# Attention with a window, then a gated feed-forward: earlier requests for V and q/k, weights between casts, inverse sums first

## The chip, the cores and the metric

The kernel runs on one core of a Trainium2 chip. The metric is the device time of one execution in microseconds, as the median of several runs. A core has four computing engines that run side by side and meet at semaphores: TensorE (PE, matrix products; its weight loads are listed apart as PEld), VectorE (DVE), ScalarE (ACT) and GpSimd (POOL). SyncE (SP) only asks for transfers. ScalarE and GpSimd can ask for transfers too. [...]

## The reference

There are 4 batches of 8 heads, 768 positions and 64 values per head. A query sees the 128 positions up to its own and the first 4 positions ("sinks"). The heads' outputs are put side by side as 512 columns and go through a gated feed-forward.

```python
scores = scale * np.matmul(q, k.transpose(0, 1, 3, 2))
keep = is_sink | in_window            # pos < 4, or 0 <= i - j < 128
a = np.exp(where(keep, scores, -1e9) - max)
a = a / (sum(a) + 1e-09)
x = matmul(a, v)                      # -> (3072, 512)
out = (maximum(x @ w_gate, 0) * (x @ w_val)) @ w_out   # 512 -> 1536 -> 512
```

All inputs and the output are float32. The kernel computes in bfloat16 with float32 sums.

## The kernel before

Two heads form a pair; a batch has 4 pairs, `U[0]` to `U[3]` for batch 0. For a pair the kernel does three things:

- **T**: transposes q and k on TensorE (for batch 0 in halves of 384 positions, `T_half(c)`: `c` 0 to 3 are the first halves of pairs 0 to 3, 4 to 7 the second halves) and copies them out of PSUM.
- **S**: scores, `Sg(u, s)`, for a group `s` of query blocks, exp on ScalarE and, where no bias was added, a mask product on VectorE. Groups 0 and 3 serve the first half of the positions, 4 and 2 the second half, in batch 0.
- **V**: `V(u, part)`, for a half of the positions: sums of the exps (weights `ones`), the weighted sums over V (weights `vn`), the inverse, and the product of both into `xT`.

V has 7 row blocks `j`; part 0 needs `j` 0 to 2 and 16 rows of 3, part 1 needs 2 to 6. The first part of the program is the *head*: everything up to the first half of the positions of batch 0, all 4 pairs.

```python
def load_half(c, queues=(nc.sync, nc.sync)):     # asks for half c of k and of q
def cast_half(c, copies=(gpsimd, gpsimd)):       # to bfloat16, k and q
def gate_half(c):
    nc.gpsimd.memset(half(kf, c)[0:1, 0:2], 0.0) # the load that follows waits for GpSimd to get here
def load_w(m0, m1):                              # one request each for w_gate and w_val, on GpSimd's queue
...
def T_half(c):
    t, x = c % NP, c // NP
    if c <= NP:
        both = pair()                            # one PSUM tile for k and q
        tk, tq = both[:, 0, :], both[:, 1, :]
    else:
        tk, tq = G[3][:, 0:256], G[3][:, 256:512]
    ... 6 transposes (line 260), key copies on ScalarE (line 266)
    (nc.scalar.copy if c in (2, 3, 4) else nc.vector.tensor_copy)(qT..., vq)     # line 267

def V(u, part, between=None):
    pv, pd = two()
    ...
    sums(pd, lambda j, h: ones[:])               # line 301
    if between:
        between()
    sums(pv, lambda j, h: vn[u.b % 2][:, j, 2 * u.p + h, :])   # line 301
    nc.vector.transpose(out=t1[:], in_=pd[:, 0:CUT])           # line 312
    nc.vector.reciprocal(r[:], ...)
    nc.vector.transpose(out=R..., in_=r...)
    nc.vector.tensor_tensor(xT..., pv[:, 0:CUT], R[:], op=Alu.mult)   # line 316
...
# the head, its second half
V(U[0], 0, lambda: T_half(2))
cast_half(3, (nc.gpsimd.tensor_copy, nc.scalar.copy))
Sg(U[2], 0)
load_w(0, 2)
V(U[1], 0)
Sg(U[2], 3)
T_half(3)
cast_half(4)
V(U[2], 0)
Sg(U[3], 0)
cast_half(5)
Sg(U[3], 3)
for c in (6, 7):
    gate_half(c)
    load_half(c)
load_w(2, 4)
T_half(4)
V(U[3], 0)
load_w(4, 6)
Sg(U[0], 4)
T_half(5)
Sg(U[0], 2)
spin(3, 2)                                       # idle matmuls that keep TensorE going
```

Behind the head come 96 *slots*, 24 for each batch: a slot is one chunk `(b, g, m)` of the feed-forward's first layer, that is 4 matmuls for the gate (line 328), relu on ScalarE, 4 matmuls for the value (line 333) and a product on VectorE into `hT` (line 335). Chunk `m` uses weights `m`. Behind each chunk stand the pieces of attention that the plan gives to its slot, and three matmuls of the second layer (line 348) where they are ready. Ahead of each chunk stands what `prep` gives to its slot: casts and requests.

```python
for s, w in {0: "S14 S12", 2: "H2", 3: "S24 S22 H3", 5: "S34 S32", 6: "V01", 7: "V11", 8: "V21", 9: "V31"}.items():
    ...                       # S14: Sg of pair 1, group 4; H2: second half of pair 2 transposed; V01: pair 0, part 1
for s, w in {11: "T0", 12: "T1", 13: "S00 S01", ..., 22: "V30 S02"}.items():   # batch 1
    ...
prep[0] += [("half", 6), ("lv0",), ("w", 6, 8), ("half", 7), ("w", 8, 10)]     # casts of halves 6, 7; weights
prep[2] += [("v", 0, j) for j in (3, 4, 5, 6)]                                 # casts of V 3 to 6
prep[3] += [("w", 10, 12)]
prep[7] += [("load", 4), ("load", 5), ("load", 6), ("lv", 1)]                  # loads of batch 1
```

Here `lv0` first writes two values of each of V's blocks 3 to 6 on GpSimd, so that the requests for them, on SyncE, wait for GpSimd to get to this place.

Of the kernel before, what the change touches and what calls it, by code (L numbers as in the profile page):

```python
# [19 lines left out]
def kernel(  # L20
# [12 lines left out]
    nc = tc.nc  # L33
    B, H, S, D = q.shape
    assert (B, H, S, D) == (4, 8, 768, 64)
    NP = H // 2
# [13 lines left out]
    NQ, NE, NT = 3, 4, 4  # L50
# [34 lines left out]

    V2 = [(4, 2, 0, 255, 112), (5, 2, 255, 399, 240), (6, 2, 399, 419, 364)]
    VSEG = [[(0, 0, 0, 247, 0), (1, 0, 247, 499, 120), (2, 1, 0, 140, 244), (3, 1, 255, 267, 372)],
            [(2, 1, 140, 255, 0), (3, 1, 267, 507, 0)] + V2]
    VSEG0 = [[(0, 0, 0, 247, 0), (1, 0, 247, 499, 120), (2, 1, 0, 140, 244), (3, 1, 140, 152, 372)],
             [(2, 1, 152, 267, 0), (3, 1, 267, 507, 0)] + V2]  # L90

    class Unit:
        def __init__(self, i):
# [2 lines left out]
    U = [Unit(i) for i in range(B * NP)]  # L96
# [15 lines left out]
    def cast_half(c, copies=(nc.gpsimd.tensor_copy, nc.gpsimd.tensor_copy)):  # L112
        for src, dst, copy in ((kf, kn, copies[0]), (qf, qn, copies[1])):
            copy(half(dst, c).rearrange("p (n h d) -> p h n d", n=3, h=2),
                                  half(src, c).rearrange("p (h n d) -> p h n d", n=3, h=2))

    def gate_half(c):
        nc.gpsimd.memset(half(kf, c)[0:1, 0:2], 0.0)


    VROW = [0, 116, 244, 368, 496, 620, 748]
# [52 lines left out]
    def setup():  # L174
        nc.vector.memset(warm[:], 0.0)
        nc.scalar.activation(warm[:], warm[:], Act.Exp, bias=0.0, scale=1.0)
        make_identity(nc, ident)

        nc.gpsimd.memset(band[:], 1.0)
        nc.gpsimd.affine_select(out=band[:], in_=band[:], compare_op=Alu.is_ge, fill=0.0, base=0,  # L180
                                pattern=[[1, 256]], channel_multiplier=-1)
        nc.gpsimd.affine_select(out=band[:], in_=band[:], compare_op=Alu.is_ge, fill=0.0, base=127,
                                pattern=[[-1, 256]], channel_multiplier=1)
        nc.gpsimd.affine_select(out=msk[:, 0, 0:247], in_=band[:, 0:247], compare_op=Alu.is_ge, fill=0.0,
                                base=119, pattern=[[0, 247]], channel_multiplier=-1)
        cp, ms = nc.vector.tensor_copy, nc.vector.memset
        for i in range(NT):
            ms(kE[i][:, 120:124], 0.0)
            ms(kE[i][:, 396:508], 0.0)
            ms(kE[i][:, 784:896], 0.0)  # L190
        ms(ones[:], 1.0)
        ms(vn[0][:, 3, :, :], 0.0)
        cp(msk[:, 0, 247:499], band[:, 4:256])
        ms(msk[0:4, 0, 247:499], 1.0)
        ms(msk[0:4, 0, 0:120], 1.0)
        ms(msk[0:4, 0, 120:247], 0.0)
        bias(mb[:, 0, 0:499], msk[:, 0, 0:499])
        bias(mb[:, 1, 0:140], band[:, 0:140])
        bias(mb[:, 1, 140:152], band[:, 4:16])
        ms(mb[0:4, 1, 140:152], 0.0)  # L200
        ms(vf[:, 6, :, :], 0.0)

    def bias(dst, src):
        nc.vector.tensor_scalar(dst, src, -1.0, BIG, op0=Alu.add, op1=Alu.mult)

    def setup2():
        cp, ms = nc.vector.tensor_copy, nc.vector.memset
        for g, w in ((1, 252), (2, 144)):
            cp(msk[:, g, 0:255], band[:, 0:255])
            cp(msk[:, g, 255:255 + w], band[:, 4:4 + w])  # L210
            ms(msk[0:4, g, 255:255 + w], 1.0)
        cp(msk[:, 2, 399:419], band[:, 0:20])

    rot, srot = [0], [0]
    head = [True]
# [34 lines left out]

    def T_half(c):
        t, x = c % NP, c // NP
        if c <= NP:
            both = pair()
            tk, tq = both[:, 0, :], both[:, 1, :]
        else:
            tk, tq = G[3][:, 0:256], G[3][:, 256:512]
        for src, ps in ((kn, tk), (qn, tq)):
            for n in range(3):
                nc.tensor.transpose(ps.bitcast(BF16)[:, 128 * n:128 * n + 128], half(src, c)[:, 128 * n:128 * n + 128],  # L260
                                    ident[:])
        vk, vq = (ps.bitcast(BF16)[:, 0:HALF].rearrange("d (n p) -> d p n", p=128) for ps in (tk, tq))
        e = kE[t]

        for r0, r1, c0 in ((0, 40, 0), (40, 124, 128), (124, 128, 384)) if x == 0 else ((0, 80, 396), (80, 128, 640)):
            nc.scalar.copy(e[:, c0:c0 + 3 * (r1 - r0)].rearrange("d (p n) -> d p n", n=3), vk[:, r0:r1])
        (nc.scalar.copy if c in (2, 3, 4) else nc.vector.tensor_copy)(
            qT[t][:, x * HALF:x * HALF + HALF].rearrange("d (p n) -> d p n", n=3), vq)
        if x == 0:
            sinks(U[t], nc.scalar.copy)  # L270
# [20 lines left out]

    ready = {}

    def V(u, part, between=None):
        pv, pd = two()
        segs = (VSEG if u.b else VSEG0)[part]

        def sums(out, w):
            for i, (j, g, c0, c1, o0) in enumerate(segs):
                for h in range(2):  # L300
                    nc.tensor.matmul(out=out[64 * h:64 * h + 64, o0:o0 + c1 - c0], lhsT=w(j, h),  # L301
                                     rhs=ee[u.i % NE][:, g, h, c0:c1], start=i == 0, stop=i == len(segs) - 1,
                                     skip_group_check=True)

        sums(pd, lambda j, h: ones[:])
        if between:
            between()
        sums(pv, lambda j, h: vn[u.b % 2][:, j, 2 * u.p + h, :])
        t1 = npool.tile([128, CUT], F32, name="t1")
        R = npool.tile([128, CUT], F32, name="R")  # L310
        r = npool.tile([128, CUT // 32], F32, name="r")
        nc.vector.transpose(out=t1[:], in_=pd[:, 0:CUT])  # L312
        nc.vector.reciprocal(r[:], t1[:].rearrange("p (c e) -> p c e", e=32)[:, :, 0])
        nc.vector.transpose(out=R[:].rearrange("p (c e) -> p c e", e=32),  # L314
                            in_=r[:].unsqueeze(2).to_broadcast([128, CUT // 32, 32]))
        nc.vector.tensor_tensor(xT[u.b % 2][:, u.p, CUT * part:CUT * part + CUT], pv[:, 0:CUT], R[:], op=Alu.mult)  # L316
        ready[u.b, u.p, part] = True

    gvn = [0]

# [34 lines left out]
    with tc.manual_schedule():  # L355
# [9 lines left out]
        for c in range(3, 6):  # L365
            load_half(c)
        setup()
        cast_half(0)
        T_half(0)
        spin(5)  # L370
        cast_half(1)
        T_half(1)
        setup2()
        Sg(U[0], 0)
        Sg(U[0], 3)
        cast_v(0, 0)
        spin(2)
        Sg(U[1], 0)
        cast_v(0, 3, 16, nc.vector.tensor_copy)
        cast_half(2)  # L380
        cast_v(0, 1)
        cast_v(0, 2)
        Sg(U[1], 3)
        V(U[0], 0, lambda: T_half(2))
        cast_half(3, (nc.gpsimd.tensor_copy, nc.scalar.copy))
        Sg(U[2], 0)
        load_w(0, 2)
        V(U[1], 0)
        Sg(U[2], 3)
        T_half(3)  # L390
        cast_half(4)
# [1 line left out]
        Sg(U[3], 0)  # L393
        cast_half(5)
        Sg(U[3], 3)
        for c in (6, 7):
            gate_half(c)
            load_half(c)
        load_w(2, 4)
        T_half(4)  # L400
        V(U[3], 0)
        load_w(4, 6)
        Sg(U[0], 4)
        T_half(5)
        Sg(U[0], 2)
        spin(3, 2)
        head[0] = False


# [8 lines left out]
            at[st] = s  # L418
            plan[s].append(st)

        for s, w in {0: "S14 S12", 2: "H2", 3: "S24 S22 H3", 5: "S34 S32", 6: "V01", 7: "V11", 8: "V21",
                     9: "V31"}.items():
            for y in w.split():
                put(s, y, 0)
        for s, w in {11: "T0", 12: "T1", 13: "S00 S01", 14: "S10 S11", 15: "T2", 16: "S20 S21", 17: "V00", 18: "V10",
                     19: "T3", 20: "V20", 21: "S30 S31", 22: "V30 S02"}.items():
            for y in w.split():
                put(s, y, 1)
        for b in range(2, B + 1):
# [5 lines left out]
            for x, y in enumerate(w.split()):  # L435
                put(24 * (b - 1) + x // 2 * 2, y[0] + y[2:], b - (y[1] == "p"))
        prep = [[] for _ in slots]
        prep[0] += [("half", 6), ("lv0",), ("w", 6, 8), ("half", 7), ("w", 8, 10)]
        prep[2] += [("v", 0, j) for j in (3, 4, 5, 6)]
        prep[3] += [("w", 10, 12)]  # L440
        prep[7] += [("load", 4), ("load", 5), ("load", 6), ("lv", 1)]
        prep[9] += [("kq", 4)]
        prep[10] += [("load", 7), ("kq", 5)]
        prep[13] += [("kq", 6)]
        prep[14] += [("v", 1, j) for j in range(7)]
        prep[16] += [("kq", 7), ("td", 8), ("wo",)]
        for i in range(ND, len(U)):
            t = at["S", i - NP, 2] + 1
# [12 lines left out]
        for s, (b, g, m) in enumerate(slots):  # L461
            for x in prep[s]:
# [12 lines left out]
                elif x[0] == "td":  # L475
                    to_dram(U[x[1]])
                elif x[0] == "turn":
                    turn(U[x[1]])
                elif x[0] == "sinks":
                    sinks(U[x[1]], nc.gpsimd.tensor_copy)  # L480
                elif x[0] == "lv0":
                    for j in (3, 4, 5, 6):
                        nc.gpsimd.memset(vf[32:33, j, 0, 0:2], 0.0)
                        load_v(0, j, 16 if j == 3 else 0)
                elif x[0] == "lv":
                    for j in range(7):
                        load_v(x[1], j)
                else:
                    cast_v(*x[1:])
# [55 lines left out]
```

The softmax here doesn't subtract the row's maximum and nothing guards it: scores larger than these inputs give would overflow.

## Time and profile before

| | |
|---|---|
| time, median of 3 | 265.59 us (265.55 to 266.02) |
| span of the profiled execution | 264.3 us |
| start of chunk 0 | 20.51 us |
| TensorE, busy | 249.9 us, 95% |
| VectorE, ScalarE, GpSimd, busy | 149.1, 117.4, 74.0 us |
| Sync queue (q1), moved | 21.83 MB |
| GpSimd queue (q0), moved | 7.87 MB |
| granted TensorE clock, mean | 0.986 |

In a line of a timeline the columns are: start, duration, engine, line of the program, instruction, what it writes and reads with shapes, and how many instructions are merged; in brackets the idle time ahead of it and what ended that. A wait for several things is put down to the one that came last by the profile, which is sometimes not the true one. "Busy" of PE and PEld overlap.

### The profile page before, as it was taken

What the parts mean: (1) busy time and instruction counts of PE and PEld (TensorE: products, weight loads), DVE (VectorE), ACT (ScalarE), POOL (GpSimd) and SP (SyncE); (2) the same over time, 40 slices, a digit from 0 to 9 for tenths busy, and PEclk for the clock granted to TensorE, in tenths of its full rate; (3) what the DMA queues carried; (4) which work ended last, traced back from release to release, by engine and by line L of the source; (5) the groups of instructions that cost most, each with busy time, mean ns of one, the idle gap of its engine ahead of it and who ended that gap; (6) DMA issues with size and microseconds to landing.
All of it is one profiled execution on the core that took longest, in us unless ns stands there. A gap on an engine that the chain in (4) does not pass through costs nothing.

```text
span 264.3 us, 5502 instructions
## 1 busy us (share of the span) xinstructions
PE 249.9 (95%) x2145; PEld 140.6 (53%) x2145; DVE 149.1 (56%) x314; ACT 117.4 (44%) x226; POOL 74.0 (28%) x106
## 2 busy tenths in 40 slices
PE   7889939998989999999999999999999999999994
PEld 3465515655646555555555555555555655555441
DVE  5577718777986774666537667657355642322000
ACT  3777802386353535553434355464344233332211
POOL 6687135299920014694000044000000000000000
PEclk9999968999999999999999999999999999999999
DMA  7999999939999259499412395310110111001232
GB/s 191 255 192 215 189 300 278 190 120 71 191 169 140 56 134 198 97 166 160 93 46 62 61 218 112 93 40 2 40 42 0 42 40 41 28 16 40 79 122 79
DMA packets 81266, 30.45 MB, mean 115 GB/s; under 512 B 65368, under 2 KB 77144, under 8 KB 81240
## 3 DMA queue, kind: packets, MB, share of 16 engines
q1 hardware_dynamic: 47944, 21.83, 33.3%
q0 software_dynamic: 32752, 7.87, 31.8%
q8 instruction: 17, 0.28, 0.5%
q10 hardware_dynamic: 544, 0.39, 0.5%
q14 instruction: 9, 0.07, 0.1%
HBM read 28.48 MB, written 9.44 MB: 143 GB/s over the span
## 4 chain that ended last, share of the span: by engine, by line
PE 77%; DMA 9%; DVE 4%; POOL 3%; issue 2%; SPq 2%; ACT 2%; ACTq 0%; POOLq 0%; DVEq 0%
PE g L348 21%; PE g L328 21%; PE g L333 20%; PE pp L301 7%; DMA vf<-in_v_dram 6%; PE pp L348 4%; PE pp L282 4%; DMA qf<-in_q_dram 4%; SPq L130 2%; DVE hT L335 1%; PE pp L240 1%; POOL vn L134 1%; DVE qT L248 1%; ACT ee L286 1%; DVE R L314 1%
## 5 line engine op out<-in xcount | busy, mean ns | idle before, releaser
L335 DVE TENSOR_TENSOR hT<-gs,g 128x384 bf16<-128x384 f32 x96 | 52.9, 551 | 64.9 <-PE g L333 63.1
L331 ACT ACTIVATE gs<-g 128x384 f32<-128x384 f32 x96 | 47.4, 494 | 76.9 <-PE g L328 75.7
L333 PE MATMUL g<-xT,wv 128*128 128x384 bf16 x384 | 78.8, 328 | 1.0 <-ACT ee L286 0.6
L328 PE MATMUL g<-xT,wg 128*128 128x384 bf16 x384 | 79.0, 328 | 0.0
L348 PE MATMUL g<-wo,hT 128*128 128x512 bf16 x240 | 64.1, 380 | 0.0
L286 ACT ACTIVATE ee<-pp 128x998 bf16<-128x998 f32 (+4 forms) x52 | 45.7, 903 | 31.3 <-PE pp L282 31.0
L328 PEld LDWEIGHTS <-wg 128*128 128x128 bf16 x384 | 36.1, 98 | 31.7 <-issue 1.2
L333 PEld LDWEIGHTS <-wv 128*128 128x128 bf16 x384 | 37.5, 98 | 27.1 <-DMA wv<-in_moe_w_val_dram 2.1
L348 PEld LDWEIGHTS <-hT 128*128 128x128 bf16 x288 | 26.2, 98 | 26.2 <-issue 2.1
L289 DVE TENSOR_TENSOR ee<-ee,msk 128x838 bf16<-128x838 bf16 (+4 forms) x48 | 29.3, 619 | 8.8 <-ACT ee L286 8.6
L134 POOL CAST vn<-vf 128x512 bf16<-128x512 f32 x28 | 17.8, 653 | 39.6 <-DMA vf<-in_v_dram 39.6
L151 POOL DMA_DIRECT2D qd<-in_q_dram x8 | 25.1, 4248 | 0.0
L151 POOL DMA_DIRECT2D kd<-in_k_dram x8 | 22.7, 3676 | 0.3 <-issue 0.3
L312 DVE STREAM_TRANSPOSE t<-pp 128x384 f32<-128x384 f32 x28 | 16.3, 581 | 8.9 <-PE pp L301 8.3
L352 ACT COPY ot<-g 128x512 f32<-128x512 f32 x20 | 11.7, 585 | 18.2 <-PE g L348 17.4
L282 PE MATMUL pp<-qT,kE 64*128 64x255 bf16 (+6 forms) x240 | 17.4, 246 | 2.0 <-DVE qT L248 1.0
L314 DVE STREAM_TRANSPOSE R<-r 128x384 f32<-128x384 f32 x32 | 18.5, 578 | 1.1
L301 PE MATMUL pp<-ee,vn 128*64 128x115 bf16 (+8 forms) x256 | 14.5, 236 | 4.2 <-POOL vn L134 4.2
L301 PEld LDWEIGHTS <-ones 128*64 128x64 bf16 x288 | 12.3, 110 | 9.7 <-issue 9.4
L316 DVE TENSOR_TENSOR xT<-pp,R 128x384 bf16<-128x384 f32 x28 | 15.6, 557 | 1.0
L301 PEld LDWEIGHTS <-vn 128*64 128x64 bf16 x288 | 12.5, 111 | 5.5 <-POOL vn L134 5.4
L301 PE MATMUL pp<-ee,ones 128*64 128x115 bf16 (+8 forms) x256 | 14.5, 239 | 0.1
(76 smaller groups left out, 126.7 us busy)
## 6 DMA issues: line engine op xcount, KB each, us to landing
out_dram<-ot SPq DMA_DIRECT2D x24, 256.0 KB
vf<-in_v_dram SPq DMA_DIRECT2D x12, 256.0 KB
vf<-in_v_dram SPq DMA_DIRECT2D x12, 224.0 KB
kf<-in_k_dram SPq DMA_DIRECT2D x8, 192.0 KB
wg<-in_moe_w_gate_dram POOLq DMA_DIRECT2D x6, 256.0 KB, 7.2
wv<-in_moe_w_val_dram POOLq DMA_DIRECT2D x6, 256.0 KB, 8.9
kf<-in_k_dram SPq DMA_DIRECT2D x4, 384.0 KB
qf<-in_q_dram SPq DMA_DIRECT2D x4, 384.0 KB
```

Of the source, the lines that this page charges most:

```text
L134: copy(flat(vn[b % 2][0:rows, j, :, :]), flat(vf[0:rows, j, :, :]))
L151: nc.gpsimd.dma_start(out=dst[u.i - ND].rearrange("s (h d) -> s h d", h=2), in_=x[u.b, 2 * u.p:2 * u.p + 2].rearrange("h s d -> s h d"))
L282: nc.tensor.matmul(out=ps[:, h, c0:c1], lhsT=kE[t][64 * h:64 * h + 64, x0:x0 + 128], rhs=qT[t][64 * h:64 * h + 64, q0:q0 + c1 - c0], start ...
L286: nc.scalar.activation(x, ps[:, :, b0:n], Act.Exp, bias=0.0, scale=scale)
L289: nc.vector.tensor_tensor(x, x, msk[:, g, m0:m0 + c1 - c0].unsqueeze(1).to_broadcast([128, 2, c1 - c0]), op=Alu.mult)
L301: nc.tensor.matmul(out=out[64 * h:64 * h + 64, o0:o0 + c1 - c0], lhsT=w(j, h), rhs=ee[u.i % NE][:, g, h, c0:c1], start=i == 0, stop=i == l ...
L314: nc.vector.transpose(out=R[:].rearrange("p (c e) -> p c e", e=32), in_=r[:].unsqueeze(2).to_broadcast([128, CUT // 32, 32]))
L328: nc.tensor.matmul(out=gp[:, 0:CUT], lhsT=wg[:, ko, m * 128:(m + 1) * 128], rhs=x[:, ko, c], start=ko == 0, stop=ko == KO - 1)
L331: nc.scalar.activation(gs[:], gp[:, 0:CUT], Act.Relu, bias=0.0, scale=1.0)
L333: nc.tensor.matmul(out=vp[:, 0:CUT], lhsT=wv[:, ko, m * 128:(m + 1) * 128], rhs=x[:, ko, c], start=ko == 0, stop=ko == KO - 1)
L335: nc.vector.tensor_tensor(h[:, m, c], gs[:], vp[:, 0:CUT], op=Alu.mult)
L348: nc.tensor.matmul(out=op, lhsT=hT[b % 2][:, m, t * 128:(t + 1) * 128], rhs=wo[:, m, :], start=m == 0, stop=m == FM - 1)
```

## The change

The gates in front of the second halves of pairs 2 and 3 (halves 6 and 7) and in front of V's blocks 3 to 6 are taken out: SyncE asks for all of them in the head, straight behind what it asked for before. GpSimd's casts of them and its requests for the weights from 6 on now stand in one list, in turns, so that the weights don't all go out at once beside V. In the head, `V` is cut in four steps, so that the inverse of the sums of pairs 0 and 1 can be computed before the weighted sums, which have to wait for V. The scores of pair 0 move ahead of the transposes of half 1; the transposes of halves 0 and 1 get two separate PSUM tiles; the copies of q of pairs 2 and 3 go from ScalarE to VectorE. What the head did of the second halves (the scores of pair 0 and the transposes of half 5) moves behind chunk 0. The plan of batch 0 from there on is one slot earlier, and the first pieces of batch 1 are one slot later, with the pieces V10 and T3 in one slot.

```diff
# the renaming of V2 to VLAST is cut
@@ -113,9 +113,6 @@
         for src, dst, copy in ((kf, kn, copies[0]), (qf, qn, copies[1])):
             copy(half(dst, c).rearrange("p (n h d) -> p h n d", n=3, h=2),
                                   half(src, c).rearrange("p (h n d) -> p h n d", n=3, h=2))
-
-    def gate_half(c):
-        nc.gpsimd.memset(half(kf, c)[0:1, 0:2], 0.0)
 
 
     VROW = [0, 116, 244, 368, 496, 620, 748]
@@ -190,6 +187,7 @@
             ms(kE[i][:, 784:896], 0.0)
         ms(ones[:], 1.0)
         ms(vn[0][:, 3, :, :], 0.0)
+        ms(vf[:, 6, :, :], 0.0)
         cp(msk[:, 0, 247:499], band[:, 4:256])
         ms(msk[0:4, 0, 247:499], 1.0)
         ms(msk[0:4, 0, 0:120], 1.0)
@@ -198,18 +196,18 @@
         bias(mb[:, 1, 0:140], band[:, 0:140])
         bias(mb[:, 1, 140:152], band[:, 4:16])
         ms(mb[0:4, 1, 140:152], 0.0)
-        ms(vf[:, 6, :, :], 0.0)
 
     def bias(dst, src):
         nc.vector.tensor_scalar(dst, src, -1.0, BIG, op0=Alu.add, op1=Alu.mult)
 
-    def setup2():
+    def setup2(g):
         cp, ms = nc.vector.tensor_copy, nc.vector.memset
-        for g, w in ((1, 252), (2, 144)):
-            cp(msk[:, g, 0:255], band[:, 0:255])
-            cp(msk[:, g, 255:255 + w], band[:, 4:4 + w])
-            ms(msk[0:4, g, 255:255 + w], 1.0)
-        cp(msk[:, 2, 399:419], band[:, 0:20])
+        w = (0, 252, 144)[g]
+        cp(msk[:, g, 0:255], band[:, 0:255])
+        cp(msk[:, g, 255:255 + w], band[:, 4:4 + w])
+        ms(msk[0:4, g, 255:255 + w], 1.0)
+        if g == 2:
+            cp(msk[:, 2, 399:419], band[:, 0:20])
 
     rot, srot = [0], [0]
     head = [True]
@@ -250,7 +248,9 @@
 
     def T_half(c):
         t, x = c % NP, c // NP
-        if c <= NP:
+        if c < 2:
+            tk, tq = two()
+        elif head[0]:
             both = pair()
             tk, tq = both[:, 0, :], both[:, 1, :]
         else:
@@ -264,7 +264,7 @@
 
         for r0, r1, c0 in ((0, 40, 0), (40, 124, 128), (124, 128, 384)) if x == 0 else ((0, 80, 396), (80, 128, 640)):
             nc.scalar.copy(e[:, c0:c0 + 3 * (r1 - r0)].rearrange("d (p n) -> d p n", n=3), vk[:, r0:r1])
-        (nc.scalar.copy if c in (2, 3, 4) else nc.vector.tensor_copy)(
+        (nc.scalar.copy if c == 4 else nc.vector.tensor_copy)(
             qT[t][:, x * HALF:x * HALF + HALF].rearrange("d (p n) -> d p n", n=3), vq)
         if x == 0:
             sinks(U[t], nc.scalar.copy)
@@ -291,21 +291,22 @@
 
     ready = {}
 
-    def V(u, part, between=None):
+    def sums(u, part, out, w):
+        segs = (VSEG if u.b else VSEG0)[part]
+        for i, (j, g, c0, c1, o0) in enumerate(segs):
+            for h in range(2):
+                nc.tensor.matmul(out=out[64 * h:64 * h + 64, o0:o0 + c1 - c0], lhsT=w(j, h),
+                                 rhs=ee[u.i % NE][:, g, h, c0:c1], start=i == 0, stop=i == len(segs) - 1,
+                                 skip_group_check=True)
+
+    def V1(u, part):
+
         pv, pd = two()
-        segs = (VSEG if u.b else VSEG0)[part]
-
-        def sums(out, w):
-            for i, (j, g, c0, c1, o0) in enumerate(segs):
-                for h in range(2):
-                    nc.tensor.matmul(out=out[64 * h:64 * h + 64, o0:o0 + c1 - c0], lhsT=w(j, h),
-                                     rhs=ee[u.i % NE][:, g, h, c0:c1], start=i == 0, stop=i == len(segs) - 1,
-                                     skip_group_check=True)
-
-        sums(pd, lambda j, h: ones[:])
-        if between:
-            between()
-        sums(pv, lambda j, h: vn[u.b % 2][:, j, 2 * u.p + h, :])
+        sums(u, part, pd, lambda j, h: ones[:])
+        return u, part, pv, pd
+
+    def V2(u, part, pv, pd):
+
         t1 = npool.tile([128, CUT], F32, name="t1")
         R = npool.tile([128, CUT], F32, name="R")
         r = npool.tile([128, CUT // 32], F32, name="r")
@@ -313,8 +314,19 @@
         nc.vector.reciprocal(r[:], t1[:].rearrange("p (c e) -> p c e", e=32)[:, :, 0])
         nc.vector.transpose(out=R[:].rearrange("p (c e) -> p c e", e=32),
                             in_=r[:].unsqueeze(2).to_broadcast([128, CUT // 32, 32]))
+        return u, part, pv, R
+
+    def V3(u, part, pv):
+        sums(u, part, pv, lambda j, h: vn[u.b % 2][:, j, 2 * u.p + h, :])
+
+    def V4(u, part, pv, R):
         nc.vector.tensor_tensor(xT[u.b % 2][:, u.p, CUT * part:CUT * part + CUT], pv[:, 0:CUT], R[:], op=Alu.mult)
         ready[u.b, u.p, part] = True
+
+    def V(u, part):
+        x = V1(u, part)
+        V3(*x[:3])
+        V4(*V2(*x))
 
     gvn = [0]
 
@@ -365,27 +377,33 @@
         for c in range(3, 6):
             load_half(c)
         setup()
+        setup2(1)
         cast_half(0)
         T_half(0)
-        spin(5)
+        spin(2, 1)
+        Sg(U[0], 0)
+        Sg(U[0], 3)
         cast_half(1)
         T_half(1)
-        setup2()
-        Sg(U[0], 0)
-        Sg(U[0], 3)
         cast_v(0, 0)
-        spin(2)
+        cast_v(0, 3, 16, nc.vector.tensor_copy)
+        x = V1(U[0], 0)
+        v0 = V2(*x)
         Sg(U[1], 0)
-        cast_v(0, 3, 16, nc.vector.tensor_copy)
         cast_half(2)
         cast_v(0, 1)
         cast_v(0, 2)
         Sg(U[1], 3)
-        V(U[0], 0, lambda: T_half(2))
+        T_half(2)
+        x = V1(U[1], 0)
+        v1 = V2(*x)
+        V3(*v0[:3])
+        V4(*v0)
+        V3(*v1[:3])
+        V4(*v1)
         cast_half(3, (nc.gpsimd.tensor_copy, nc.scalar.copy))
         Sg(U[2], 0)
         load_w(0, 2)
-        V(U[1], 0)
         Sg(U[2], 3)
         T_half(3)
         cast_half(4)
@@ -393,17 +411,16 @@
         Sg(U[3], 0)
         cast_half(5)
         Sg(U[3], 3)
-        for c in (6, 7):
-            gate_half(c)
-            load_half(c)
         load_w(2, 4)
+        load_half(6)
+        load_half(7)
+        for j in (3, 4, 5, 6):
+            load_v(0, j, 16 if j == 3 else 0)
+        V(U[3], 0)
         T_half(4)
-        V(U[3], 0)
+        setup2(2)
         load_w(4, 6)
-        Sg(U[0], 4)
-        T_half(5)
-        Sg(U[0], 2)
-        spin(3, 2)
+        spin(6, 2)
         head[0] = False
 
 
@@ -418,12 +435,12 @@
             at[st] = s
             plan[s].append(st)
 
-        for s, w in {0: "S14 S12", 2: "H2", 3: "S24 S22 H3", 5: "S34 S32", 6: "V01", 7: "V11", 8: "V21",
-                     9: "V31"}.items():
+        for s, w in {0: "S04 S02 H1", 1: "S14 S12", 2: "H2", 3: "S24 S22 H3", 4: "S34 S32", 5: "V01", 6: "V11",
+                     7: "V21", 8: "V31"}.items():
             for y in w.split():
                 put(s, y, 0)
-        for s, w in {11: "T0", 12: "T1", 13: "S00 S01", 14: "S10 S11", 15: "T2", 16: "S20 S21", 17: "V00", 18: "V10",
-                     19: "T3", 20: "V20", 21: "S30 S31", 22: "V30 S02"}.items():
+        for s, w in {12: "T0", 13: "T1", 14: "S00 S01", 15: "S10 S11", 16: "T2", 17: "S20 S21", 18: "V00",
+                     19: "V10 T3", 20: "V20", 21: "S30 S31", 22: "V30 S02"}.items():
             for y in w.split():
                 put(s, y, 1)
         for b in range(2, B + 1):
@@ -435,14 +452,12 @@
             for x, y in enumerate(w.split()):
                 put(24 * (b - 1) + x // 2 * 2, y[0] + y[2:], b - (y[1] == "p"))
         prep = [[] for _ in slots]
-        prep[0] += [("half", 6), ("lv0",), ("w", 6, 8), ("half", 7), ("w", 8, 10)]
-        prep[2] += [("v", 0, j) for j in (3, 4, 5, 6)]
-        prep[3] += [("w", 10, 12)]
-        prep[7] += [("load", 4), ("load", 5), ("load", 6), ("lv", 1)]
-        prep[9] += [("kq", 4)]
-        prep[10] += [("load", 7), ("kq", 5)]
+        prep[1] += [("half", 6), ("half", 7), ("v", 0, 3), ("v", 0, 4), ("w", 6, 8), ("v", 0, 5), ("v", 0, 6),
+                    ("w", 8, 10), ("w", 10, 12)]
+        prep[9] += [("load", 4), ("load", 5), ("load", 6), ("lv", 1)]
+        prep[10] += [("kq", 4), ("load", 7), ("kq", 5)]
         prep[13] += [("kq", 6)]
-        prep[14] += [("v", 1, j) for j in range(7)]
+        prep[15] += [("v", 1, j) for j in range(7)]
         prep[16] += [("kq", 7), ("td", 8), ("wo",)]
         for i in range(ND, len(U)):
             t = at["S", i - NP, 2] + 1
@@ -478,10 +493,6 @@
                     turn(U[x[1]])
                 elif x[0] == "sinks":
                     sinks(U[x[1]], nc.gpsimd.tensor_copy)
-                elif x[0] == "lv0":
-                    for j in (3, 4, 5, 6):
-                        nc.gpsimd.memset(vf[32:33, j, 0, 0:2], 0.0)
-                        load_v(0, j, 16 if j == 3 else 0)
                 elif x[0] == "lv":
                     for j in range(7):
                         load_v(x[1], j)
```

More of the change, by code (lines that the diff above doesn't have):

```diff
@@ L84 @@
            4: (1, 152, 507, [(252, 384, 152, 267), (380, 384, 267, 507)])}
-    V2 = [(4, 2, 0, 255, 112), (5, 2, 255, 399, 240), (6, 2, 399, 419, 364)]
+    VLAST = [(4, 2, 0, 255, 112), (5, 2, 255, 399, 240), (6, 2, 399, 419, 364)]
     VSEG = [[(0, 0, 0, 247, 0), (1, 0, 247, 499, 120), (2, 1, 0, 140, 244), (3, 1, 255, 267, 372)],
-            [(2, 1, 140, 255, 0), (3, 1, 267, 507, 0)] + V2]
+            [(2, 1, 140, 255, 0), (3, 1, 267, 507, 0)] + VLAST]
     VSEG0 = [[(0, 0, 0, 247, 0), (1, 0, 247, 499, 120), (2, 1, 0, 140, 244), (3, 1, 140, 152, 372)],
-             [(2, 1, 152, 267, 0), (3, 1, 267, 507, 0)] + V2]
+             [(2, 1, 152, 267, 0), (3, 1, 267, 507, 0)] + VLAST]
     class Unit:
```

## The prediction

> **What bounds the kernel now.** I read five views, from the coarse to the fine. First the first part of the page, busy time by engine:
>
> ```profile
> PE 249.9 (95%) x2145; PEld 140.6 (53%) x2145; DVE 149.1 (56%) x314; ACT 117.4 (44%) x226; POOL 74.0 (28%) x106
> ```
>
> TensorE is busy for 249.9 of 264.3 us, so time can be won only where it idles or runs slowly. Second, the slices of the page, to find that place:
>
> ```profile
> PE   7889939998989999999999999999999999999994
> ...
> PEclk9999968999999999999999999999999999999999
> ```
>
> A slice is 6.6 us. The first four are the head; the sixth (33 to 39.6 us) is the hole: PE 3 tenths, and in it and the next the granted clock falls to 6 and 8 tenths. Third, who waits for whom on PE:
>
> ```profile
> PE pp L301 <- POOL vn L134: 4.2, 3, 2.6
> ...
> PE pp L260 <- ACT ee L286: 1.0, 2, 0.7
> ...
> PE g L333 <- DMA wv<-in_moe_w_val_dram: 0.3, 1, 0.3
> ```
>
> The columns are the total in us, the number of waits and the longest. Line 301 with vn as weights is the weighted sum over V, and line 134 the GpSimd cast of V. Fourth, the timeline of 30.5 to 39.5 us, all engines:
>
> ```profile
> 30.59 0.61 POOL L134 CAST vn<-vf 128x512 bf16<-128x512 f32 x1 [3.92 <-DMA vf<-in_v_dram]
> ...
> 32.57 0.44 PEld L333 LDWEIGHTS <-wv 128*128 128x128 bf16 x4 [1.01 <-DMA wv<-in_moe_w_val_dram]
> 32.58 0.82 PE L333 MATMUL g<-xT,wv 128*128 128x384 bf16 x4 [0.63 <-ACT ee L286]
> ...
> 33.33 0.54 PE L301 MATMUL pp<-ee,ones 128*64 128x115 bf16 x10
> ...
> 35.43 0.43 PE L301 MATMUL pp<-ee,vn 128*64 128x255 bf16 x2 [1.39 <-POOL vn L134]
> ...
> 37.78 1.17 POOL L134 CAST vn<-vf 128x512 bf16<-128x512 f32 x2 [2.41 <-DMA vf<-in_v_dram]
> 38.45 0.33 PE L301 MATMUL pp<-ee,vn 128*64 128x144 bf16 x2 [2.59 <-POOL vn L134]
> ```
>
> PE waits for the cast, the cast for the V rows 3 to 6 of batch 0, which land at about 30.5, 34.7 and 37.7 us. At 32.58 the wait is put down to ScalarE, but the weight load just before it waited for wv: weights 6 to 8, asked for at 23.19 us, land only then, 9.4 us later. So weights too arrive just in time. Last, the DMA engines by stretches of 2 us (last columns: granted clock, share, GB/s):
>
> ```profile
> 14.00:16.00 2.00, 2.00 (x33) 1.34 (x32) 1.83 (x5) 1.64 (x7) 2.00 (x7) 1.00 1.02 136
> 16.00:18.00 2.00, 1.32 (x20) 0.87 (x18) 1.52 (x4) 1.44 (x3) 2.00 (x3) 1.00 1.34 213
> ...
> 28.00:30.00 2.00, 2.00 (x16) 1.19 (x13) 1.51 (x4) 1.89 (x5) 0.00 (x0) 1.00 1.35 189
> ...
> 36.00:38.00 2.00, 0.00 (x0) 0.00 (x0) 0.00 (x0) 0.00 (x0) 0.22 (x1) 0.50 1.06 331
> ```
>
> From 16 to 34 us both queues are full and move about 205 GB/s together (mean of the stretches, 182 to 225). At 14 to 16 us only weights move, 136 GB/s: the Sync queue had nothing to do, because the gates held back halves 6 and 7 until 15.9 us, and V 3 to 6 until 22.4 us.
>
> **What the Trainium skill says.** "DMA: Bandwidth & Descriptors", section "Issuing engines are not separate DMA queues": requests of Sync, ScalarE and GpSimd all run on the same 16 engines and interleave. The trace agrees: a Sync queue beside the weights lifts 136 to 213 GB/s, not to a sum of two full streams. So asking earlier makes no bandwidth; it only fills the 2 idle us and changes the order. The same page, section "Specifications", puts the least transfer for line rate at 512 B; the V rows here are 64 floats, 256 B, and the stretches with V and weights are the slowest (182 to 189 GB/s). "TensorE: Matmul & The Clock Gate", section "What's actually happening": an idle array falls to half clock until it has been busy for a while. The trace agrees: 0.50 at 36 to 38 us, and eight matmuls of a chunk then take 2.67 us (39.17 to 41.84) for 1.31.
>
> **The change part by part.**
>
> *Head.* The Scores of pair 0 go ahead of the transposes of half 1, the copies of q for pairs 0 to 3 go to VectorE, and separate PSUM tiles let the two copies of halves 0 and 1 run side by side. I followed the chain by hand with the durations of the timeline (ScalarE key copies 0.60, exp pair 1.3 to 1.5, VectorE inverse 1.4, q copy 0.56, matmul groups 0.3 to 0.6). The exps of pair 0 start near 6.6 instead of 7.54 us, and pair 0's inverse is ready at 9.9 instead of 12.1. But the weighted sums of pairs 0 and 1 still need V 1 and 2, cast at 10.72 to 11.93 behind a DMA, and the Scores of pair 2 stand behind them on PE. Pair 2's exps start near 13.3 (13.14 before), pair 3's near 16.3 (16.29 before), and pair 3's VectorE chain, 18.30 to 20.43 before, starts at about 18.15. Chunk 0 starts at about 20.36 instead of 20.51: 0.15 us won. The early gain dies at a transfer.
>
> *Work moved behind the head.* Two Scores of pair 0 (18.86 and 19.56 us, about 0.3 each) and six transposes (19.12, 0.35) ran in PE's wait for pair 3's inverse. They now run in slot 0, where PE is the bound; idle matmuls take their place. Cost: 0.95 us.
>
> *Slots 0 to 9.* From the timeline a slot costs 1.40 us with other work behind it, 1.31 without, plus 0.45 for a pair's Scores, 0.35 for transposes, 0.84 for a V. Before, these add to 19.2 us for slots 0 to 9, but the trace takes 20.51 to 47.24, 26.7 us. The 7.5 us between are: the V of slot 6 (5.84 us from 33.33 to 39.17 for 0.84) 5.0; the slow clock in chunk 7, 1.36, and in the next V (0.92 for 0.84), 0.1; the two weight waits 0.63 and 0.30. That is 7.4, and about 0.1 is rounding; another 0.2 is lost to the last weights at 48.1 us. So 7.7 us could go.
>
> *DMA after.* Sync's queue runs on from 14 us without a gate: halves 6 and 7 (4 x 192 KB) and V 3 to 6 (224+256+256+40 KB), 1.58 MB. Beside it go weights 0 to 6 on GpSimd's queue. Estimate: with some 115 GB/s for Sync (halves 6 and 7 took about 16.3 to 23 us for 0.79 MB) all V is there by about 28 to 29.5 us. The first late V now runs in slot 5: 20.36 + 2.35 + 1.84 + 1.75 + 2.19 + 1.85 + 1.40 = 31.7 us. So the wait for V goes. But weights 6 to 8 are now asked for after the cast of V 4, about 26 instead of 22.45. Chunk 6 wants them at 32.6 (wg) and 33.2 us (wv). Everything up to them, 1.58 + 8 x 0.262 = 3.68 MB less some 0.2 moved before 14 us, at 200 GB/s ends at 31.4, and the landing lags. I take 0.6 us of wait here. Weights 2 to 4 were the wait of 0.30 at 24.77; they have a fuller queue beside them now and are wanted only 0.7 us later. I take 0.8 us. Together 1.4 us given back.
>
> *Slots 12 to 22.* The batch-1 chain starts a slot later and has one slot less up to slot 20 (V of pair 1 and the transposes of pair 3 share slot 19). VectorE is busy without a break from 64.5 to 76.5 us, and PE waits 0.73 us for it at 73.86 now. With one slot of 1.4 us less to hide it, and one product of 0.5 us less in it, I take 0.5 us more of that wait.
>
> *Sum.* -7.7 + 0.95 - 0.15 + 1.4 + 0.5 = -5.0 us; a few tenths are likely to be lost at handovers, so -4.8: 265.6 - 4.8 = 260.8 us.
>
> **The rivals.**
>
> *A: the wait moves from V to the weights.* For it: weights 6 to 8 landed exactly when wanted while they were asked for 3.5 us earlier. If they land 9.4 us after 26.5 us, at 36, PE waits 2.8 us, and may see the slow clock: 263 to 264.5 us. Against it: V 3 to 6, which ran beside them, is then nearly through, and the shortest landing of wv in the trace is 5.5 us.
>
> *B: the weights are early enough and nothing takes the place of the wait.* For it: the idle stretch at 14 to 16 us is used, and the order matches the needs better (weights 8 to 10 no longer run before V 5). Then only 0.95 + 0.5 of the 7.7 are lost: 259 us, or 258.3 with a better head.
>
> *C: batch 1 comes late.* Its loads are asked for at slot 9 (about 37 to 38 us) where ScalarE had already asked at 32.8 us, PE standing still. Two transposes of 3 KB rows want kq 4 at about 45 us. The cast takes 2 x 0.84, so it must land by 43. Mixed with the last weights 0.79 MB needs 3 to 5 us: in time, barely. If not, 1 to 1.5 us more.
>
> **Range and chances.** A and C make 262 to 264.5, B 258.3 to 259, and my middle is 260.8. Hence 258.3 to 263.8 for 8 in 10. The 2% line is at 260.28, inside the range and a little under the middle: 0.39 faster, 0.58 within, 0.03 slower. Slower than 270.9 would need a new stall longer than the one removed.
>
> **What would show it.** Right: no wait of line 301 for line 134 over 0.5 us after 25 us; the late V of pair 0 at 31 to 33 us; PEclk 9 in every slice; chunk 0 within 0.4 us of 20.4; the waits that are left are weight loads for wg or wv in slots 2 to 6, under 2 us together; VectorE's wait before the Scores of pair 3 in batch 1 at 1.0 to 1.5 us. Wrong: a weight wait over 2 us with a clock dip (A), transposes of batch 1 waiting for a cast (C), or chunk 0 outside 19.5 to 21 us, which would say that my chain through the head is not the one that binds.

## The result and the profile after

| | before | after |
|---|---|---|
| time, median | 265.80 us (265.55 to 266.21) | 264.04 us (263.58 to 264.27) |
| ratio, 95% interval | 1 | 0.993 (0.991 to 0.995) |
| span of the profiled execution | 264.3 us | 261.9 us |
| chunk 0 starts | 20.51 us | 19.92 us |
| first late V (V01) starts, ends | 33.33, 39.17 us | 33.99, 34.83 us |
| first transposes of batch 1 (T0) | 50.16 us, behind chunk 11 | 47.55 us, behind chunk 12 |
| second layer starts (in slot 24) | 80.83 us | 77.75 us |

The change wins 1.8 us. My sum was 5.0 us won, and a little less with handovers, 260.8 us; the time lies 0.2 us above the range that I gave. The hole itself went as foreseen. First the page of the changed kernel, busy time and slices:

```profile
PE 247.7 (95%) x2143; PEld 140.5 (54%) x2143; DVE 151.2 (58%) x316; ACT 116.5 (44%) x224; POOL 73.0 (28%) x100
...
PE   7877899998899999999999999999999999999994
...
PEclk9999999999999999999999999999999999999998
```

The slice with 3 tenths has gone, and the clock stays at 9 tenths up to the last slice. But the fourth and fifth slices (20 to 33 us, 6.55 us each) stand at 7 and 8 tenths. Who PE waits for, from 19 us to the end, says why (total in us, times, longest):

```profile
PE pp L282 <- DVE qT L267: 1.7, 2, 0.9
PE pp L282 <- DVE qT L246: 1.0, 2, 0.7
PE pp L282 <- DVE xT L323: 0.8, 1, 0.8
PE g L345 <- DMA wv<-in_moe_w_val_dram: 0.7, 1, 0.7
PE pp L238 <- DVE xT L323: 0.7, 1, 0.7
PE g L340 <- DVE hT L347: 0.5, 1, 0.5
PE pp L298 <- POOL vn L131: 0.5, 1, 0.5
```

(The lines have moved: 298, the sums of V, was 301; 340 and 345, the gate and value matmuls of a chunk, were 328 and 333; 347, the product into `hT`, was 335; 323, the product into `xT`, was 316; 131, the cast of V, was 134. Lines 238 and 246 are the transposes and the copy of q from batch 1 on, before 240 and 248; 282, the scores, and 267, the copy of q in batch 0, kept their numbers.) The kernel before, for the second and third entries:

```profile
PE pp L282 <- DVE qT L248: 1.0, 2, 0.7
PE pp L282 <- DVE xT L316: 0.7, 1, 0.7
```

So these two are not new. The wait of 4.2 us for the cast of V in batch 0 is gone; the 0.5 us in the last entry is in batch 2. The fourth entry, for the value weights of chunk 0, is new at this place: of waits for value weights the kernel before had 0.3 and 0.63 us, elsewhere. New too are the first and the last three. Of the 4.1 us of new waits VectorE makes 2.9, in the first, fifth and sixth entries, so it is VectorE and not a transfer that cost most here. The timeline of PE shows where:

```profile
21.47 0.82 PE L345 MATMUL g<-xT,wv 128*128 128x384 bf16 x4 [0.74 <-DMA wv<-in_moe_w_val_dram]
...
25.27 0.51 PE L282 MATMUL pp<-qT,kE 64*128 64x115 bf16 x10 [0.79 <-DVE qT L267]
...
32.14 0.52 PE L282 MATMUL pp<-qT,kE 64*128 64x115 bf16 x10 [0.95 <-DVE qT L267]
...
33.99 0.54 PE L298 MATMUL pp<-ee,ones 128*64 128x115 bf16 x10
...
44.86 0.81 PE L340 MATMUL g<-xT,wg 128*128 128x384 bf16 x4 [0.54 <-DVE hT L347]
...
65.08 0.57 PE L238 MATMUL pp<-ident,kn 64*64 64x64 bf16 x24 [0.69 <-DVE xT L323]
```

And around the first wait for qT, VectorE and ScalarE in the timeline of all engines:

```profile
22.85 0.33 PE L260 MATMUL g<-ident,qn 128*128 128x128 bf16 x3
...
24.00 0.55 ACT L266 COPY kE<-g 128x240 bf16<-128x240 bf16 x2
24.15 0.60 DVE L289 TENSOR_TENSOR ee<-ee,msk 128x838 bf16<-128x838 bf16 x1 [0.15 <-ACT ee L286]
...
24.66 0.55 DVE L267 COPY qT<-g 128x384 bf16<-128x384 bf16 x1
```

The transposes of half 5 were done at 23.2 us. Their copies stand in both queues behind the scores of the same slot: on ScalarE behind two exps (to 24.1), on VectorE behind the mask products that need those exps (to 24.7). So the copy of q ends at 25.2, and the scores of slot 1, which need it, wait 0.79 us. In slots 3 and 4 the same happens with half 7. ("One slot earlier" in the description of the change holds for batch 0 from the scores of pair 3 on; those of pair 1 stand one slot later than before, right behind the transposes that they need.)

### The profile page after: what moved, and what is told of

Same layout as the page of the kernel before. It is cut to its first block, busy times and chain, and to the rows that moved or that the text cites. A ratio compares the mean times of both kernels' runs of the same rounds, so it can differ in the third digit from the quotient of the medians.

```text
span 261.9 us, 5490 instructions
## 1 busy us (share of the span) xinstructions
PE 247.7 (95%) x2143; PEld 140.5 (54%) x2143; DVE 151.2 (58%) x316; ACT 116.5 (44%) x224; POOL 73.0 (28%) x100
## 4 chain that ended last, share of the span: by engine, by line
PE 74%; DMA 8%; DVE 7%; ACT 3%; issue 3%; SPq 2%; POOL 1%; DVEq 0%; ACTq 0%
PE g L360 20%; PE g L340 19%; PE g L345 19%; PE pp L298 7%; DMA vf<-in_v_dram 5%; PE pp L360 4%; PE pp L282 4%; DMA wv<-in_moe_w_val_dram 3%; ACT ee L286 3%; SPq L127 2%; DVE hT L347 2%; DVE t L313 1%; DVE R L315 1%; DVE ee L289 1%; DVE qT L246 1%
## 5 line engine op out<-in xcount | busy, mean ns | idle before, releaser
L289 DVE TENSOR_TENSOR ee<-ee,msk 128x838 bf16<-128x838 bf16 (+4 forms) x48 | 30.0, 633 | 10.7 <-ACT ee L286 10.6
L282 PEld LDWEIGHTS <-kE 64*128 64x128 bf16 x240 | 8.8, 94 | 11.8 <-issue 8.4
L298 PE MATMUL pp<-ee,vn 128*64 128x115 bf16 (+8 forms) x256 | 13.9, 233 | 0.5 <-POOL vn L131 0.5
```

What stands on the lines that cost most here:

```text
L282: nc.tensor.matmul(out=ps[:, h, c0:c1], lhsT=kE[t][64 * h:64 * h + 64, x0:x0 + 128], rhs=qT[t][64 * h:64 * h + 64, q0:q0 + c1 - c0], start ...
L289: nc.vector.tensor_tensor(x, x, msk[:, g, m0:m0 + c1 - c0].unsqueeze(1).to_broadcast([128, 2, c1 - c0]), op=Alu.mult)
```

## The experiments

My theory O was that the requests earn what I had predicted, and that the order of the new plan gives it back on VectorE. Rival D was that the fuller queue costs it, by late weights. Medians and ranges hold every run; the ratios with intervals leave out runs over 1.5% above the shortest of the same kernel. The kernel before, timed again beside them, took 265.88 to 265.98 us in the median.

**1 and 5: only the requests.** The kernel before, with its own head and plan:

```diff
-for c in (6, 7):
-    gate_half(c)
-    load_half(c)
 load_w(2, 4)
+load_half(6); load_half(7)
+for j in (3, 4, 5, 6): load_v(0, j, 16 if j == 3 else 0)
 ...
-prep[0], prep[2], prep[3] of before
+prep[0] += half 6, half 7, v 3, v 4, w 6-8, v 5, v 6, w 8-10, w 10-12
```

> The kernel before, with only the requests of the change: no gates, halves 6 and 7 and V 3 to 6 asked for in the head, casts and weights in turns. Head and plan stay. Theory O (order: the requests earn the 5 us hole at 33 to 39 us, and what is missing was given back by VectorE's program order in the new plan): no wait of line 301 for V, no wait for a copy of q, chunk 0 near 20.5, 259.5 to 261.5 us, faster than the whole change. Rival D (transfers: the fuller queue makes weights land late, and that is what the missing time is): new waits for wg or wv of over 1.5 us together, 263 us or more.

Measured: median 262.99, but from 259.79 to 267.82 us; ratio 0.981 (0.975 to 0.986). The profiled run was the shortest, 258.0 us of span: no wait for V, none over 0.3 us for a copy of line 267 after 19 us, weight waits of 0.29 and 0.62 us, T0 at 43.89. The median lies above the range of theory O, yet the one profile shows none of what rival D asked for. So the requests alone can win 6 us, but not in every run. The same kernel again:

> The same kernel as the first experiment (only the requests of the change), with more runs, because its time spread from 259.8 to 267.8 us. Theory O: the median is below that of the whole change, 260 to 263 us, and runs that are longer have a new wait behind slot 24, for V of batch 2. Rival D: longer runs wait for weights or V between 20 and 40 us.

260.05 to 267.79 us, median 265.91; ratio 0.978 (0.974 to 0.982). Neither expectation of the place was met: the profiled run, a long one, waited neither in batch 2 nor before 40 us, but at chunk 10:

```profile
45.81 1.46 PE L333 MATMUL g<-xT,wv 128*128 128x384 bf16 x4 [3.31 <-DMA wv<-in_moe_w_val_dram]
```

These are the last weights, asked for at 33.65 us and landed 12.1 us later, where the short run of the same kernel had 7.7 us as its longest landing for value weights. The slow clock follows (1.46 us for 0.82).

**2: copies of q first.** In slots 0 and 3 the transposes go ahead of the scores:

```diff
-0: "S04 S02 H1", ... 3: "S24 S22 H3"
+0: "H1 S04 S02", ... 3: "H3 S24 S22"
```

> The changed kernel, with the transposes of halves 5 and 7 put ahead of the scores in slots 0 and 3, so that VectorE copies q before the mask products. Theory O: the waits of 0.79 and 0.95 us before the scores of slots 1 and 4 go, the first late V starts at about 32.3 instead of 33.99, and 1 to 1.7 us are won: 262.3 to 263 us. Rival D: the weights 6 to 8, asked for at 27 to 28.6 us, are then the bound; the late V starts earlier but chunk 6 waits for them, and the time stays at 263.7 to 264.2.

Both waits went, and chunk 6 doesn't wait for weights in their place. The time is 263.44 us (261.63 to 268.08), ratio 0.988 (0.983 to 0.992), against 0.993; the intervals overlap, so the times alone don't show a gain. The profiled run was the longest, and even in it the stretch from chunk 0 to chunk 10 takes 21.5 us (20.46 to 41.96) for 22.9. It lost its time later, with 2.7 us of waits for V of batch 2, three in a row, and the slow clock behind them:

```profile
104.76 0.23 PE L298 MATMUL pp<-ee,vn 128*64 128x12 bf16 x2 [1.00 <-POOL vn L131]
104.92 0.61 PE L282 MATMUL pp<-qT,kE 64*128 64x255 bf16 x4
105.45 1.46 PE L360 MATMUL g<-wo,hT 128*128 128x512 bf16 x3
```

So the last weights of experiment 5 are not the only thing that makes a run long.

**3: batch 1 as before.**

```diff
-12: "T0", 13: "T1", ... 18: "V00", 19: "V10 T3"
+11: "T0", 12: "T1", ... 17: "V00", 18: "V10", 19: "T3"
-prep[9] += loads of batch 1
+prep[7] += loads of batch 1
```

> The changed kernel, with the plan of batch 1 and its loads as in the kernel before: transposes from slot 11, loads asked for at slot 7, V10 and T3 in slots of their own. Theory O: the wait of 0.54 before chunk 11 and that of 0.69 before the transposes of pair 3 go: 262.6 to 263.3 us. Rival D: the loads of batch 1 at slot 7 meet the last weights, chunk 8 or 10 waits for wg or wv, or the transposes of slot 11 wait for kq 4: 264 us or more.

262.82 us (262.69 to 262.96), ratio 0.988 (0.985 to 0.990). The wait of 0.69 before the transposes of pair 3 and that of 0.49 for V of batch 2 went, together 1.2 us, as much as the medians differ. (The profiled executions differ by 0.8 us, since in this one the waits for q were 0.4 us longer and that for weights 0 to 2 was 0.3 us longer.) The wait of 0.54 before chunk 11 stayed, so its cause was not the place of T0, as I had thought. Chunk 11 writes the bank that chunk 9's product must empty. With V31 in slot 8, that product stands behind V31's inverse on VectorE (it runs at 44.27 in the changed kernel); with V31 in slot 9 it stood ahead of it, and the kernels below that put V31 back there (8 to 11) don't have this wait.

**4: both.**

> The two edits together. Theory O: they add, 260.8 to 262 us, with no PE wait over 0.5 us between chunk 1 and the first transposes of batch 1 but for weights. Rival D: no better than the better one of the two alone; a wait for weights or for kq 4 of over 1 us stands in the place of the others.

262.21 us (261.62 to 264.77), ratio 0.987 (0.982 to 0.992). The intervals of experiments 2, 3 and 4 overlap, so whether the two add can't be told from the times; the profile shows what each does. From the start of chunk 0 to that of chunk 10 it takes 19.86 to 41.33, 21.5 us, where the changed kernel takes 19.92 to 42.86, 22.9 us: 1.5 of the 1.74 us of waits for q were won. Then:

```profile
44.01 0.82 PE L345 MATMUL g<-xT,wv 128*128 128x384 bf16 x4 [1.86 <-DMA wv<-in_moe_w_val_dram]
```

Rival D is right here, for one wait: weights 10 to 12 again, landing after 10.1 us. It also covers the wait before chunk 11.

**6: V of batch 2 early.** On the kernel of experiment 1, `("lv", 2)` moves from slot 27 to slot 17.

> Requests only, and V of batch 2 asked for at slot 17 instead of slot 27, ahead of the transposing transfers on the Sync queue. If V of batch 2 makes the spread (the changed kernel waits 0.49 us for its cast at 102.95 us, a run of the second experiment 2.7 us), it goes: 259 to 261 us in every run. If the spread comes from elsewhere, it stays; if the early V holds up the transfers that make q and k of batch 2, the time is 262 us or more.

259.75 to 268.97 us, median 263.17, ratio 0.981 (0.976 to 0.987). The spread stayed, so the late request for V of batch 2 is not what makes it in this kernel. The profiled run waited nowhere for V, but 1.82 us for w_out at 80.2 us, which was not so in experiment 1, and 2.3 us for the value weights of chunks 0 and 2.

**7: the gates back.** The changed kernel with gates, weights and casts of the kernel before.

> The changed kernel with the requests of the kernel before: gates, weights 6 to 10 ahead of V, casts of V in slot 2. Head and plan are the changed ones. Theory O: the wait for V is back, even longer since it comes a slot earlier, with the slow clock: 266 to 268.5 us, slower than the kernel before. Rival D (the requests cost as much as they bring): 264 to 265 us.

269.63 us (268.61 to 276.17), ratio 1.013 (1.009 to 1.016): slower than before, and above the range expected. PE's waits from 19 us:

```profile
PE pp L298 <- POOL vn L131: 5.1, 5, 2.0
PE pp L282 <- DVE qT L267: 1.8, 2, 0.9
```

The wait for V in batch 0 is back with 3.9 us (before 4.2, so it is not longer, as I had thought); the other 1.2 us are in batch 2. So the new head and plan without the requests cost 3.7 us (269.63 for 265.93), and in them the requests are worth 269.63 - 264.04 = 5.6 us.

**8: the plan back.** The changed kernel, with the plan and the batch-1 loads of the kernel before and this end of the head:

```diff
-spin(6, 2)
+Sg(U[0], 4)
+T_half(5)
+Sg(U[0], 2)
+spin(3, 2)
```

> The changed kernel with the whole plan of the kernel before, the scores of pair 0 and the transposes of half 5 back in the head: requests and the new head, no new plan. If the new head is worth the 0.4 to 0.6 us by which chunk 0 starts earlier, 259.2 to 261 us in undisturbed runs, 0.5 less than the requests alone; if its gain dies (half 5 then ends later, or weights 0 are late), the same as the requests alone or slower.

261.59 us (260.50 to 268.78), ratio 0.983 (0.979 to 0.986). The second branch came true: the gain of the head dies. With this end of the head the scores of pair 0 wait 1.01 us for the q of half 4 (0.29 before), whose transposes now stand behind V of pair 3, and the slow clock follows. Chunk 0 starts at 22.66 in its profile, 2.7 us later than in the changed kernel. Yet chunk 11 starts at 43.30 for 44.86, 1.6 us earlier: no wait for weights, none for q and none for the product of chunk 9 stands between.

**9 to 11: the last weights.** On experiment 8, first with the loads of batch 1 split, then with weights ahead of casts, then with both. In 10, weights 6 to 8 go out one cast earlier and 8 to 10 two casts; 10 to 12 stay behind V 6, but no longer behind 8 to 10:

```diff
# 9
-prep[7] += load 4, load 5, load 6, lv 1
+prep[7] += load 4;  prep[9] += load 5, load 6, lv 1
# 10
-v 3, v 4, w 6-8, v 5, v 6, w 8-10, w 10-12
+v 3, w 6-8, v 4, w 8-10, v 5, v 6, w 10-12
```

> The kernel of the eighth experiment, with only pair 0 of batch 1 asked for at slot 7; pairs 1 and 2 and V of batch 1 at slot 9. Theory W: the longer runs of the experiments with the old plan wait for the last weights (10 to 12, asked for near 33 us, wanted near 41 to 43), since the loads of batch 1 pass them on the shared DMA engines; one such run waited 3.31 us at 45.8 and then had the slow clock. Then the split takes the spread away: all runs 260 to 262.5 us. Rival V (the spread comes from later, V of batch 2 or the transposing transfers): runs over 265 us remain.

261.45 us (260.94 to 264.43), ratio 0.985 (0.981 to 0.990): less spread, but two of six runs, 262.83 and 264.43, above what I had expected.

> The kernel of the eighth experiment, with each pair of late weights one cast earlier: 6 to 8 behind the cast of V 3, 8 to 10 behind that of V 4, 10 to 12 behind that of V 6. Theory W: weights 10 to 12 are asked for 1.5 us earlier and find their queue emptier, so fewer or no runs over 263 us, 260 to 262 us in the median; V 5 and 6 land up to 2 us later, still ahead of 34 us. Rival V: the spread stays as it was.

261.17 us (260.48 to 261.19) in five runs, ratio 0.981 (0.978 to 0.984): the narrowest range of the kernels with the old plan. But the ratio can't be told from the 0.983 of experiment 8, and there one run in six was long; if one in six is the rule, five runs without a long one come about 4 times in 10. So that the spread has gone is not shown. The last weights were asked for at 32.42 us, hardly earlier than in experiment 8 (32.70), but the pair ahead of them had left at 27.05 instead of 31.24. What the order does to the transfers shows in the DMA columns (the last two, share and GB/s) of the stretches: the changed kernel, then experiment 8, then experiment 10.

```profile
28.00:30.00 2.00, 1.89 (x24) 1.31 (x22) 1.44 (x3) 1.29 (x4) 0.62 (x1) 1.00 1.03 128
...
32.00:34.00 2.00, 1.86 (x20) 1.08 (x19) 1.15 (x4) 1.49 (x3) 2.00 (x4) 1.00 0.21 15
```

```profile
28.00:30.00 2.00, 2.00 (x25) 1.27 (x24) 1.16 (x3) 1.39 (x4) 0.10 (x1) 1.00 1.25 161
...
32.00:34.00 2.00, 2.00 (x20) 1.17 (x19) 1.71 (x6) 1.54 (x3) 2.00 (x3) 1.00 0.71 80
```

```profile
28.00:30.00 2.00, 2.00 (x25) 1.30 (x23) 1.18 (x3) 1.47 (x4) 0.54 (x1) 1.00 1.44 195
...
32.00:34.00 2.00, 2.00 (x21) 1.13 (x20) 0.95 (x3) 1.47 (x3) 1.90 (x3) 1.00 1.00 124
```

In the changed kernel V has landed by 30.3 us and weights 8 to 12 are asked for only from 32.04 us on, so the DMA engines move 15 GB/s at 32 to 34 us. Experiment 10 has the weights on their way in this stretch.

> Both edits together. Theory W: the steadiest of all, every run 260 to 262 us, 0.978 to 0.985 of the kernel before. Rival V: runs over 265 us remain.

260.52 us in the median, but one of six runs at 265.57 (the shortest 260.30); ratio 0.979 (0.976 to 0.982). That one run has no profile, and its cause stays open.

**12: the new plan, mended.** Experiment 4 with the weights in the order of experiment 10.

> The changed kernel with the copies of q ahead of the masks and batch 1 at its old slots (the fourth experiment), and the late weights each one cast earlier. The fourth experiment waited 1.86 us for weights 10 to 12 at 44.0 us. Theory W: that wait goes and the short plan keeps its earlier start: 259.5 to 261 us, level with or up to 1 us under the tenth experiment. Rival T (trade: with the shorter plan the first late V stands at 32.5 us, and V 5 and 6, held up by the earlier weights, are not cast by then): a wait of line 298 for V of 0.5 to 2 us appears there, 260.5 to 263 us, and a wider spread.

261.17 us (260.69 to 261.88), ratio 0.982 (0.979 to 0.984). The wait at chunk 10 went and no wait for V came in its place, so rival T falls. This is the clearest pair for the weights, one edit apart and both profiled: at 32 to 34 us the DMA engines move 151 GB/s for 60 in experiment 4, and the last weights are asked for at 32.89 us for 33.85. Experiment 4 first:

```profile
32.00:34.00 2.00, 2.00 (x29) 1.32 (x27) 1.84 (x5) 0.89 (x2) 2.00 (x4) 1.00 0.56 60
```

```profile
32.00:34.00 2.00, 2.00 (x26) 1.22 (x22) 2.00 (x6) 1.96 (x4) 1.65 (x3) 1.00 1.19 151
```

But the time, just above the range of theory W, is only level with experiment 10:

```profile
20.32 0.82 PE L340 MATMUL g<-xT,wg 128*128 128x384 bf16 x4 [0.25 <-DMA wg<-in_moe_w_gate_dram]
22.51 0.82 PE L345 MATMUL g<-xT,wv 128*128 128x384 bf16 x4 [1.37 <-DMA wv<-in_moe_w_val_dram]
...
44.66 0.81 PE L340 MATMUL g<-xT,wg 128*128 128x384 bf16 x4 [0.68 <-DVE hT L347]
```

The earlier chunk 0 waits 1.6 us for weights 0 to 2, and V31 in slot 8 holds up chunk 11 again.

## Why the prediction was wrong

Point by point, with the profiled executions:

- **The hole (7.7 us): right.** Waits for V in batch 0 and the slow clock are gone. V 5 and 6 landed at 30.3 us (estimate 28 to 29.5), still ahead of V01. Experiment 7 brings the hole back.
- **Head (0.15 us): the size was off,** 0.59 us. Chunk 0 starts at 19.86 to 20.46 us in the six profiles with this head and this end of it, and at 20.51 to 21.47 in the four with the old head, so it does start earlier. It was of no use: the value matmuls of chunk 0 waited 0.74 us for weights 0 to 2, where I had put no wait. In experiment 12 they waited 1.37.
- **Transfers (1.4 us given back): 0.74 us, and at another place.** Neither of the two waits that I had put there came, 0.8 for weights 2 to 4 and 0.6 for 6 to 8; the 0.74 are those for weights 0 to 2. That weights cost something at all as forecast is luck. The waits for q don't explain it by giving the weights time: experiment 4 has none of these, and waits for weights at chunks 0, 4 and 10 (0.58, 0.23, 1.86), not at 2 or 6. It is the last weights that run short, at chunk 10 (experiments 4 and 5), not 6 to 8 as rival A had it.
- **Slots 0 to 5: the step that failed.** I made V01's start, 31.7 us, a sum of PE durations alone. It was 33.99. Of the 2.3 us, 1.74 are the waits for q: the moved pieces cost PE 0.95 us as foreseen, but also made slots 1 and 4 depend on copies that the same plan puts behind exps and mask products. In the plan before, the scores of pair 3 had slot 4 between. Experiments 2 and 4 take these waits away by order alone. They move the copies in ScalarE's and VectorE's queue at once, so the two are not told apart. The other 0.6 us are the wait for weights 0 to 2 (0.74) and 0.25 of handovers, less the 0.44 by which chunk 0 started before 20.36.
- **Slots 12 to 22 (0.5 us): mis-sized, about 2 us.** From chunk 10 on the changed kernel takes 1.3 us more up to slot 24, and 0.7 after it. It is 0.69 before chunk 11 (42.86 + 1.31 = 44.17 to 44.86), 0.69 before the transposes of pair 3, and 0.49 for V of batch 2. The Scores of pair 3, where I had looked, wait 0.77, as before. Experiment 3 undoes the last two; the first follows V31: it is there with V31 in slot 8 (experiments 3 and 12) and not with V31 in slot 9 (8 to 11).
- **Rival C (batch 1 late): half right.** Its loads were asked for at 40.79, not 37 to 38, and casts ended later than before (59.3 for the last of V against 56.4) though PE was ahead; T0 did not wait, V of batch 2 did.

Sum, measured: -7.7 - 0.6 + 0.95 + 0.74 + 1.74 + 2.2 (2.0, and the 0.2 at chunk 10 that the hole's count holds already) = -2.7; the spans differ by 2.4 us. The rest is handovers that I can't place.

Three readings in the prediction need a correction, though the sum doesn't hang on them. The nine stretches from 16 to 34 us have a mean of 202 GB/s, not 205. VectorE's stretch from 64.5 to 76.5 us has one gap, 0.45 us at 75.3. And the slowest stretch between 14 and 34 us is the one with weights alone, 136 GB/s, so the trace doesn't show that the short rows of V slow the stretches that they are in.

What stays open: why the same request lands after at most 7.7 us in one execution and 12.1 in the next. That the long runs of experiments 5 and 8 come from the last weights is argued from one profile of them, from experiment 4, and from the narrow range of experiments 10 and 12. Experiment 2's long run waited for V of batch 2; experiment 11, with both edits, still has one long run in six, and no other long run was profiled.

## What to carry to other kernels

When a wait is taken away and the plan is packed tighter at once, cost each moved piece on every queue that it passes, not only on the bound engine: a copy behind a mask behind an exp is a chain, and one empty slot may be what hides it. Ask early for what is needed first, but don't hold the later transfers back until the earlier ones are used: the hole in experiment 4's DMA stretches (60 GB/s) was followed by a wait of 1.86 us ten us later, and experiment 12, with the weights earlier, has neither. Where the margin of a transfer is near its spread from run to run, look at the range of the times, since a median of a few runs may hide it: the request part alone had 259.8 us as its best and 267.8 as its worst. A narrow range of five or six runs is no proof either: 260.5 to 261.2 us in experiment 10, and one run of 265.6 in experiment 11, which has the same order of weights.

## What was not expected of the hardware

A transfer's time to land was steady neither between kernels nor between executions: for value weights of 256 KB the longest landing from 20 to 60 us was 7.7 us in one execution of the kernel of experiment 1 and 12.1 in another, which made the request in question 1.3 us later. And the clock fell after a single gap of 3.31 us (experiment 5): the four matmuls after it took 1.46 us for 0.82, a loss on top of the wait. It also fell after three gaps of 0.60, 1.11 and 1.00 us with two matmuls between them (experiment 2: granted clock 0.50 from 104 to 110 us), where a single gap of 1.86 us left it at 1.00 (experiment 4).
